# Sharing a router phase's smallest logit among the partitions: through TensorE, or on VectorE alone

## The chip, the cores and the metric

The kernel runs on one core of a Trainium2 chip. The metric is the device time of one execution in microseconds; of three timed runs of the kernel before the median is 709.76 us (707.22 to 710.5). Work is done by TensorE (PE; its weight loads are PEld), VectorE (DVE), ScalarE (ACT), GpSimd (POOL, which issues the gathers and scatters here) and SyncE (SP, which issues the plain loads). Each works through its own instructions in order and waits on semaphores for the others.

## The reference, cut to what matters

Attention with a causal window of 128 and a linear bias feeds a mixture of eight experts. Tokens go to experts greedily by their logits, each expert taking at most `cap` of them.

```python
x = attention(q, k, v)                  # 4608 tokens x 512
logits = x @ w_gate                     # 4608 x 8
cap = N // E                            # 576
for idx in np.argsort(-logits.flatten()):
    tok, e = idx // E, idx % E
    if assigned[tok] >= 0 or counts[e] >= cap: continue
    assigned[tok] = e; counts[e] += 1
for e in range(E):
    h = np.maximum(x[assigned == e] @ w1[e], 0.0)
    out[assigned == e] = h @ w2[e]
```

## The kernel before, in words

The first part (to about 230 us) is the attention, head pair by head pair. It is the same before and after. From then on the experts run one after another on TensorE: `layer1` (L895) multiplies the gathered tokens, split into a high and a low part (`xh`, `xl`), by the first weights; `layer2` (L924, L925, L927) multiplies the result (`hh`, `hlo`) by the second weights into `po`. Beside the matmuls ACT and DVE split each loaded weight piece `raw` into a high and a low part `hl` (L837, L839), DVE makes `hlo` (L906), POOL gathers the next expert's tokens `g` by the indices `idx` (L848) and scatters the output (L936), and TensorE transposes `g` into `pg` (L872), from which ACT and DVE make `xh` and `xl` (L875, L876).

The router does not sort. It runs in phases 0 to 7; each closes one expert. In a phase every token has a best remaining logit `b` (L490 to L497). The phase looks for the threshold above which an expert is full: between the smallest `b` (`lo`) and the last threshold (`hi`) it lays 64 steps of width `w`, marks on DVE for each token which steps it reaches (`ind`, L556, two halves), counts the marks per expert with TensorE (L580), and finds the step at which an expert fills up (L588 to L594, then L597). That is done three times, ever finer. Then come the selection, the places of the chosen tokens (L695, L715, L716) and their list `idx` (L743 to L751). All of it stands between the expert matmuls: `phase` is a generator that yields the number of slots to wait (`WAITS`), and `slot` is called between groups of expert matmuls and takes the route one yield further when the wait is over. So a phase is spread over some twenty slots, and phases run ahead of the experts by about two. The framework's scheduler then sets the final order of each engine's instructions.

The smallest `b` is known only per partition after a reduction along the free axis (L504). `ends` brings it to all partitions: TensorE transposes the column into a row in PSUM (L509), DVE reduces the row to one number (L511), multiplies it into an identity (L513), TensorE multiplies that by ones (L516, two instructions for fp32), and DVE copies the result out and negates it (L518, L520). Two yields lie in it: `WAITS[0]` = 2 slots before L509, `WAITS[1]` = 1 slot before L516. Phases 1 to 6 call it with `top` false; phase 0 calls it once with `top` true, inside the attention, and phase 7 not at all. `EARLY` says how many yields of the route are taken before the first expert's loop starts.

Of the kernel before, what the change touches and what calls it, by code (L numbers as in the profile page):

```python
# [5 lines left out]
F32 = mybir.dt.float32  # L6
# [4 lines left out]
ALU = mybir.AluOpType  # L11
AX = mybir.AxisListType
# [398 lines left out]

CONST_AT = 4
WARM, WARM0, WARM1 = 11, 16, 4
EARLY = 4
AHEAD = (18, 0, 0)
EARLY0 = 1
SOON, HI0 = 2, 1
# [4 lines left out]
WAITS = (2, 1, 3, 1, 1, 2, 3)  # L422
# [13 lines left out]
def bc(ap, shape):  # L436
    return ap.to_broadcast(shape)
# [17 lines left out]
class Router:  # L455
# [43 lines left out]
    def ends(self, b, top):  # L499

        nc, C = self.nc, self.C
        n = 2 if top else 1
        e = self.small("ext", 2)
        nc.vector.tensor_reduce(e[:, 0:1], b, AX.X, ALU.min, negate=True)  # L504
        if top:
            nc.vector.tensor_reduce(e[:, 1:2], b, AX.X, ALU.max)
        yield WAITS[0]
        ep = self.bank()
        nc.tensor.transpose(ep[0:n, 0:128], e[:, 0:n], C["ident"])  # L509
        em = self.p["rt"].tile([2, 1], F32, name="em")  # L510
        nc.vector.tensor_reduce(em[0:n], ep[0:n, 0:128], AX.X, ALU.max)  # L511
        ed = self.p["rt"].tile([2, 2], F32, name="ed")
        nc.vector.tensor_scalar(ed[0:n, 0:n], C["ident"][0:n, 0:n], em[0:n, 0:1], None, ALU.mult)  # L513
        yield WAITS[1]
        ea = self.bank()
        nc.tensor.matmul(ea[:, 0:n], C["onef"][0:n, :], ed[0:n, 0:n], start=True, stop=True)  # L516
        ev = self.small("ev", 2)
        nc.vector.tensor_copy(ev[:, 0:n], ea[:, 0:n])  # L518
        lo = self.small("lo")
        nc.vector.tensor_scalar(lo, ev[:, 0:1], -1.0, None, ALU.mult)  # L520
        if top:

            sp, ab = self.small("sp"), self.small("ab")
            nc.vector.tensor_tensor(sp, ev[:, 0:1], ev[:, 1:2], ALU.add)
            nc.vector.tensor_scalar(sp, sp, 2.0 ** -10, 1e-20, ALU.mult, ALU.add)
            nc.vector.tensor_scalar(ab, ev[:, 1:2], -1.0, ev[:, 1:2], ALU.mult, ALU.max)
            nc.vector.scalar_tensor_tensor(sp, ab, 2.0 ** -20, sp, ALU.mult, ALU.add)
            nc.vector.tensor_tensor(self.hi, ev[:, 1:2], sp, ALU.add)
            yield 0
        w = self.small("w")  # L530
        nc.vector.tensor_scalar(w, self.hi, lo[:, 0:1], 1.0 / J, ALU.subtract, ALU.mult)
        rw = self.small("rw")
        nc.vector.tensor_scalar(w, w, 1e-30, None, ALU.max)
        nc.vector.reciprocal(rw, w)
        return lo, w, rw

    def clamp(self, out, b, lo, w, c0=0, c1=NT):

        low = self.small("low")
        self.nc.vector.tensor_tensor(low, lo, w, ALU.subtract)  # L540
        self.nc.vector.tensor_scalar(out[:, c0:c1], b[:, c0:c1], self.hi[:, 0:1], low[:, 0:1], ALU.min, ALU.max)
# [445 lines left out]
def layer_moe(tc, P, C, r, x, w1, w2, out, exact):  # L987
# [23 lines left out]
    with tc.issue_after(last.ins):  # L1011
        for _ in range(EARLY - EARLY0):
            next(route)
# [130 lines left out]
```

## Time and profile before

| | |
|---|---|
| median of three runs | 709.76 us (707.22 to 710.5) |
| the profiled execution | 710.48 us, of which the span from first to last instruction is 708.7 us |
| PE busy | 677.7 us (96%) |
| DVE busy | 467.5 us (66%) |
| ACT / POOL busy | 330.7 us / 154.1 us |
| mean granted TensorE clock | 0.985 of full speed |
| chain that ended last | PE 88%, DVE 5%, DMA 3% |

The span has three parts: the attention to about 230 us with PE nearly full, a short stretch about 230 to 243 us in which router phase 0 ends and PE has little to do, and the experts from 243 us to the end, in which PE is again nearly full. A busy PE is one whose instructions follow without a gap; a router instruction between two expert matmuls is busy time too.

### The profile page before, as it was taken

What the parts mean: (1) busy time and instruction counts of PE and PEld (TensorE: products, weight loads), DVE (VectorE), ACT (ScalarE), POOL (GpSimd) and SP (SyncE); (2) the same over time, 40 slices, a digit from 0 to 9 for tenths busy, and PEclk for the clock granted to TensorE, in tenths of its full rate; (3) what the DMA queues carried; (4) which work ended last, traced back from release to release, by engine and by line L of the source; (5) the groups of instructions that cost most, each with busy time, mean ns of one, the idle gap of its engine ahead of it and who ended that gap; (6) DMA issues with size and microseconds to landing.
All of it is one profiled execution on the core that took longest, in us unless ns stands there. A gap on an engine that the chain in (4) does not pass through costs nothing.

```text
span 708.7 us, 19210 instructions
## 1 busy us (share of the span) xinstructions
PE 677.7 (96%) x7446; PEld 598.3 (84%) x7447; DVE 467.5 (66%) x1855; ACT 330.7 (47%) x991; POOL 154.1 (22%) x337
## 2 busy tenths in 40 slices
PE   7999999999993799999999999999999999999996
PEld 4998998998892598789788889988988988988986
DVE  6887887888887889689577828846764724523210
ACT  6988888898862343334233224314324324322211
POOL 4121221222130304323140131132034023011011
PEclk9999999999996899999999999999999999999999
DMA  8466565664521634527054235135134334401001
GB/s 304 136 215 188 167 205 170 193 217 151 171 85 38 203 104 163 187 90 239 31 175 151 77 105 179 54 114 175 61 119 132 122 97 139 138 20 40 8 24 49
DMA packets 35140, 92.74 MB, mean 131 GB/s; under 512 B 3808, under 2 KB 13152, under 8 KB 35040
## 3 DMA queue, kind: packets, MB, share of 16 engines
q1 hardware_dynamic: 29152, 72.55, 31.3%
q0 software_dynamic: 5888, 18.88, 8.2%
q8 instruction: 61, 1.00, 0.6%
q14 instruction: 39, 0.32, 0.1%
HBM read 72.54 MB, written 18.87 MB: 129 GB/s over the span
## 4 chain that ended last, share of the span: by engine, by line
PE 88%; DVE 5%; DMA 3%; issue 2%; POOL 1%; ACT 0%; SPq 0%; POOLq 0%; DVEq 0%
PE ph L895 28%; PE po L924 10%; PE po L925 10%; PE s L53 8%; PE po L927 8%; PE pt L53 7%; PE pt L157 6%; PE x L53 5%; PE pg L872 2%; DMA g<-x,idx 2%; PE m L580 1%; DVE u L133 1%; DMA raw<-in_w_dram 1%; DMA out_dram<-o,idx 1%; DMA rel_sb<-in_rel_dram 1%
## 5 line engine op out<-in xcount | busy, mean ns | idle before, releaser
L895 PE MATMUL ph<-xh,hl 128*128 128x288 f32 (+2 forms) x1024 | 193.1, 301 | 0.0
L895 PEld LDWEIGHTS ph<-xh,hl 128*128 128x128 f32 x1024 | 155.5, 190 | 1.0
L144 ACT ACTIVATE u<-u,mn 128x192 f32<-128x192 f32 (+2 forms) x288 | 123.9, 434 | 22.7 <-DVE mn L133 22.7
L924 PE MATMUL po<-hl,hh 128*128 128x512 f32 (+1 forms) x328 | 130.7, 399 | 0.0
L925 PE MATMUL po<-hl,hh 128*128 128x512 f32 (+1 forms) x328 | 126.4, 385 | 0.0
L901 ACT ACTIVATE hh<-ph 128x288 fp32r<-128x288 f32 (+2 forms) x128 | 46.7, 409 | 150.3 <-PE ph L895 141.3
L895 PE MATMUL ph<-xl,hl 128*128 128x288 f32 (+2 forms) x512 | 116.3, 298 | 0.0
L133 DVE CUSTOM_DVE_ANT_0 u<-s,bm 128x192 f32<-128x192 f32 x308 | 86.4, 333 | 30.2 <-PE s L53 29.8
L927 PE MATMUL po<-hl,hlo 128*128 128x512 f32 (+1 forms) x264 | 101.7, 385 | 0.0
L839 DVE TENSOR_TENSOR hl<-raw,hl 128x512 fp32r<-128x512 f32 x128 | 85.1, 684 | 15.2 <-ACT hl L837 14.4
L936 POOL DMA_INDIRECT out_dram<-o,idx x40 | 44.1, 1103 | 205.6 <-ACT o L931 120.8
L895 PEld LDWEIGHTS ph<-xl,hl 128*128 128x128 f32 x512 | 84.8, 190 | 0.1
L876 DVE TENSOR_TENSOR xl<-pg,xh 128x512 fp32r<-128x512 f32 (+1 forms) x37 | 23.7, 640 | 85.7 <-ACT xh L875 78.1
L906 DVE SCALAR_TENSOR_TENSOR hlo<-ph,hh 128x288 fp32r<-128x288 f32 (+2 forms) x128 | 49.6, 417 | 41.3 <-ACT hh L901 40.3
L837 ACT CAST hl<-raw 128x1024 fp32r<-128x1024 f32 x64 | 65.5, 1049 | 16.5 <-DMA raw<-in_w_dram 11.9
L53 PE MATMUL s<-qk 64*64 64x192 f32 (+1 forms) x1112 | 69.5, 319 | 2.8 <-DVE mn L133 2.6
L924 PEld LDWEIGHTS po<-hl,hh 128*128 128x128 f32 x328 | 61.7, 188 | 11.1
L925 PEld LDWEIGHTS po<-hl,hh 128*128 128x128 f32 x328 | 61.8, 188 | 10.7
L931 ACT COPY o<-po 128x512 f32<-128x512 f32 (+1 forms) x33 | 19.0, 574 | 96.5 <-PE po L927 62.5
L848 POOL DMA_INDIRECT g<-x,idx x40 | 44.7, 1119 | 82.5 <-PE pg L872 34.2
L927 PEld LDWEIGHTS po<-hl,hlo 128*128 128x128 f32 x264 | 49.6, 188 | 10.2
L53 PEld LDWEIGHTS s<-qk 64*64 64x64 f32 x1112 | 48.2, 132 | 8.4 <-issue 3.7
(217 smaller groups left out, 936.4 us busy)
## 6 DMA issues: line engine op xcount, KB each, us to landing
raw<-in_w_dram SPq DMA_DIRECT2D x64, 512.0 KB, 4.3
qk<-in_qk_dram SPq DMA_DIRECT2D x32, 576.0 KB, 5.0
v<-in_v_dram SPq DMA_DIRECT2D x32, 288.0 KB, 4.1
x<-xb SPq DMA_DIRECT2D x14, 512.0 KB, 3.4
x<-xb SPq DMA_DIRECT2D x8, 128.0 KB, 2.7
x<-xb SPq DMA_DIRECT2D x4, 256.0 KB, 2.1
g<-x,idx POOLq DMA_INDIRECT x40
out_dram<-o,idx POOLq DMA_INDIRECT x40
```

Of the source, the lines that this page charges most:

```text
L53: put(nc.tensor.matmul(out, w, a, start=start, stop=stop, skip_group_check=True))
L133: put(nc.vector.tensor_tensor_reduce(out=u[rows], in0=x[rows, c:c + 64 * m].rearrange("q (j k) -> q j k", k=64), in1=bm[n % NP][rows, y:y ...
L144: put(nc.scalar.activation(u, u, AF.Exp, bias=st["mn"][:, i:i + 1], scale=-1.0, accum_out=st["sm"][:, i:i + 1]))
L837: self.last = nc.scalar.copy(hl[:, 0, :], raw)
L839: nc.vector.tensor_tensor(hl[:, 1, c:c + 512], raw[:, c:c + 512], hl[:, 0, c:c + 512].bitcast(F32), ALU.subtract)
L848: nc.gpsimd.indirect_dma_start(out=g[:r, :], out_offset=None, in_=self.x, in_offset=bass.IndirectOffsetOnAxis(ap=idx[:r, h:h + 1], axis=0))
L895: nc.tensor.matmul(pp[t], w[:, a, j, fo:fo + 128], x[:, j, cut[t]:cut[t + 1]], start=(j == 0 and a == 0 and x is xh), stop=(j == 3 and a = ...
L901: nc.scalar.activation(o, pp[t], AF.Relu)
L906: nc.vector.scalar_tensor_tensor(d, pp[t][:, c0:c1], 0.0, o[:, c0:c1].bitcast(F32), ALU.max, ALU.subtract)
L924: nc.tensor.matmul(out, a, wh, start=(f == 0), stop=False)
L925: nc.tensor.matmul(out, a, wl, start=False, stop=(f == 7 and t == 4))
L927: nc.tensor.matmul(out, hl[:, f, 128 * t:128 * t + 128], wh, start=False, stop=(f == 7))
```

## The change: what it does

For `top` false, `ends` no longer goes through TensorE. The new `least` reduces `b` to one number per partition, copies it over 32 columns, lets DVE transpose the four 32x32 squares of each 32-partition group in place (so every partition holds the 32 values of its group), reduces again, and then twice takes the minimum with a copy shifted by partitions: first halves of 64 are exchanged (two copies), then quarters of 32 (four copies). The yield `WAITS[1]` is gone with the second TensorE instruction, so that each of the phases 1 to 6 is one yield and one slot shorter; `EARLY` goes from 4 to 3, since the third yield is now where the fourth was. `both_ends` is the old way, for `top` true.

```diff
-EARLY = 4
+EARLY = 3
...
-        n = 2 if top else 1
-        e = self.small("ext", 2)
-        nc.vector.tensor_reduce(e[:, 0:1], b, AX.X, ALU.min, negate=True)
...
-        yield WAITS[0]
-        ep = self.bank()
-        nc.tensor.transpose(ep[0:n, 0:128], e[:, 0:n], C["ident"])
-        em = self.p["rt"].tile([2, 1], F32, name="em")
-        nc.vector.tensor_reduce(em[0:n], ep[0:n, 0:128], AX.X, ALU.max)
-        ed = self.p["rt"].tile([2, 2], F32, name="ed")
-        nc.vector.tensor_scalar(ed[0:n, 0:n], C["ident"][0:n, 0:n], em[0:n, 0:1], None, ALU.mult)
-        yield WAITS[1]
-        ea = self.bank()
-        nc.tensor.matmul(ea[:, 0:n], C["onef"][0:n, :], ed[0:n, 0:n], start=True, stop=True)
-        ev = self.small("ev", 2)
-        nc.vector.tensor_copy(ev[:, 0:n], ea[:, 0:n])
-        lo = self.small("lo")
-        nc.vector.tensor_scalar(lo, ev[:, 0:1], -1.0, None, ALU.mult)
...
+        if not top:
+            lo = self.least(b)
+            yield WAITS[0]
+        else:
+            lo = yield from self.both_ends(b)
...
+    def least(self, b):
+
+        nc, rt = self.nc, self.p["rt"]
+        e, t = self.small("ext"), self.small("ext2", 64)
+        nc.vector.tensor_reduce(e, b, AX.X, ALU.min)
+        nc.vector.tensor_copy(t[:, 0:32], bc(e, [128, 32]))
+        nc.vector.transpose(t[:, 32:64], t[:, 0:32])
+        nc.vector.tensor_reduce(e, t[:, 32:64], AX.X, ALU.min)
+        for w in (64, 32):
+            o, lo = self.small("other"), self.small("lo")
+            for a in range(0, 128, w):
+                nc.vector.tensor_copy(o[a:a + w], e[a ^ w:(a ^ w) + w])
+            nc.vector.tensor_tensor(lo, e, o, ALU.min)
+            e = lo
+        return lo
```

The order of the instructions moves with it from the first expert on. Two places are shown. In the kernel after, line numbers below the new code are higher by 22.

DVE at the start of phase 4, before: `em`, `ed` and `ev` are L511, L513 and L518 of `ends`, `o` is expert 1's last output block, `hl` a split weight, `hlo` and `hh` the first layer of expert 2.

```order
L935 TENSOR_TENSOR o<-po,o_6675 64x512
L511 TENSOR_REDUCE em<-m 1x1
L839 TENSOR_TENSOR hl<-raw,hl 128x512
L513 TENSOR_SCALAR ed<-ident_sb,em 1x1
L839 TENSOR_TENSOR hl<-raw,hl 128x512
L906 SCALAR_TENSOR_TENSOR hlo<-ph,hh 128x288
L906 SCALAR_TENSOR_TENSOR hlo<-ph,hh 128x224
L906 SCALAR_TENSOR_TENSOR hh<-ph,hh 128x64
L518 COPY ev<-m 128x1
L839 TENSOR_TENSOR hl<-raw,hl 128x512
L520 TENSOR_SCALAR lo<-ev 128x1
```

DVE at the start of phase 4, after: `other` and `lo` are L525 and L526 of `least`, `ind` (L578) is what was L556, and `io` (L768) opens the last step of phase 3.

```order
L526 TENSOR_TENSOR lo<-lo,other 128x1
L508 TENSOR_SCALAR w<-hi,lo 128x1
L510 TENSOR_SCALAR w<-w 128x1
L511 RECIPROCAL rw<-w 128x1
L562 TENSOR_TENSOR low<-lo,w 128x1
L665 TENSOR_TENSOR low<-lo,w 128x1
L666 TENSOR_SCALAR w<-w 128x1
L563 TENSOR_SCALAR cl<-b,hi,low 128x36
L667 TENSOR_SCALAR rw<-rw 128x1
L568 TENSOR_SCALAR kq<-cl,lo,rw 128x72
L578 TENSOR_TENSOR ind<-kq,c_i_425 128x1152 x2
L768 COPY io<-m 64x20
```

The marks of phase 4 have moved from behind expert 2's first `hlo` to ahead of the last step of phase 3, two experts' stretches of work earlier than their count.

PE at the start of the same phase, before: the first layer of expert 2 (`ph`) with the transpose L509 and the multiplication L516 in it.

```order
L895 MATMUL ph<-xh,hl 128x288 x2
L509 MATMUL m<-ident_sb,ext 1x128
L895 MATMUL ph<-xh,hl 128x288 x2
L895 MATMUL ph<-xl,hl 128x288 x2
L895 MATMUL ph<-xh,hl 128x288 x4
L895 MATMUL ph<-xl,hl 128x288 x2
L895 MATMUL ph<-xh,hl 128x288 x2
L516 MATMUL m<-ed,craw 128x1
```

PE there after: the same layer is L917, and the first count is L602 (it was L580).

```order
L917 MATMUL ph<-xh,hl 128x288 x4
L917 MATMUL ph<-xl,hl 128x288 x2
L917 MATMUL ph<-xh,hl 128x288 x4
L917 MATMUL ph<-xl,hl 128x288 x2
L917 MATMUL ph<-xh,hl 128x288 x2
L602 LDWEIGHTS ind
```

The two router instructions are gone from the row, and 48 matmuls of the layer stand ahead of the first count, where it was 12, 12 and 41 before.

## Rows read from the trace of the kernel before

**Rows 1.** The page, busy time, and granted clock in 40 slices.

```profile
PE 677.7 (96%) x7446; PEld 598.3 (84%) x7447; DVE 467.5 (66%) x1855; ACT 330.7 (47%) x991; POOL 154.1 (22%) x337
PEclk9999999999996899999999999999999999999999
```

**Rows 2.** Busy time by stretches: PE, PEld, DVE, ACT, POOL, clock, DMA, GB/s.

```profile
300.00:340.00 40.00, 39.21 (x333) 35.70 (x332) 34.88 (x118) 14.32 (x26) 10.76 (x10) 1.00 0.44 146
```

**Rows 3.** Line L509: count, duration (min/median/max), first and last start.

```profile
L509 PE MATMUL m<-ident_sb,ext x6: 271/271/272, 242.9 to 487.4; 128*1 128x128 f32 x6
```

**Rows 4.** Timeline of PEld at L509 (phase 3) and L516 (phases 1, 5).

```profile
323.54 0.08 PEld L509 LDWEIGHTS m<-ident_sb,ext 128*1 128x1 f32 x1
323.67 0.30 PEld L895 LDWEIGHTS ph<-xh,hl 128*128 128x128 f32 x2
...
244.44 0.19 PEld L895 LDWEIGHTS ph<-xh,hl 128*128 128x128 f32 x1
...
245.07 0.19 PEld L895 LDWEIGHTS ph<-xl,hl 128*128 128x128 f32 x1
...
430.87 0.19 PEld L895 LDWEIGHTS ph<-xh,hl 128*128 128x128 f32 x1
431.30 0.29 PEld L516 LDWEIGHTS m<-ed,craw 1*128 1x128 f32 x2 [0.24 <-DVE ed L513]
431.61 0.19 PEld L895 LDWEIGHTS ph<-xh,hl 128*128 128x128 f32 x1
```

**Rows 5.** Timeline of PEld at phase 2, up to the transposes of expert 1's tokens.

```profile
279.69 0.19 PEld L927 LDWEIGHTS po<-hl,hlo 128*128 128x128 f32 x1
279.92 0.08 PEld L509 LDWEIGHTS m<-ident_sb,ext 128*1 128x1 f32 x1
...
284.56 0.42 PEld L872 LDWEIGHTS pg<-ident_sb,g 128*128 128x128 f32 x4 [1.83 <-DMA g<-x,idx]
```

**Rows 6.** Timeline of POOL at the gather for expert 1.

```profile
277.25 1.44 POOL L848 DMA_INDIRECT g<-x,idx  x1 [5.87 <-issue]
278.99 3.27 POOL L848 DMA_INDIRECT g<-x,idx  x1 [0.30 <-issue]
```

**Rows 7.** Timeline of DVE at the start of phase 4.

```profile
370.34 0.20 DVE L513 TENSOR_SCALAR ed<-ident_sb,em 1x1 f32<-1x1 f32 x1
...
372.72 0.46 DVE L906 SCALAR_TENSOR_TENSOR hlo<-ph,hh 128x288 fp32r<-128x288 f32 x1 [1.58 <-ACT hh L901]
...
373.87 0.15 DVE L518 COPY ev<-m 128x1 f32<-128x1 f32 x1
...
375.76 0.15 DVE L643 TENSOR_TENSOR low<-lo,w 128x1 f32<-128x1 f32 x1
375.83 0.15 DVE L644 TENSOR_SCALAR w<-w 128x1 f32<-128x1 f32 x1
...
377.06 1.42 DVE L556 TENSOR_TENSOR ind<-kq,c_i 128x1152 bf16<-128x1152 bf16 x2
```

**Rows 8.** Timeline of PEld at phase 4's first count.

```profile
377.86 0.33 PEld L580 LDWEIGHTS <-ind 128*128 128x128 bf16 x9 [1.48 <-DVE ind L556]
```

**Rows 9.** PE after that wait: length, busy time, clock, DMA share, GB/s.

```profile
379.60:383.00 3.40, 3.40 (x16) 0.50 0.47 151
```

**Rows 10.** Timeline of PE in and after that stretch.

```profile
380.40 1.16 PE L895 MATMUL ph<-xh,hl 128*128 128x288 f32 x4
381.36 0.68 PE L895 MATMUL ph<-xl,hl 128*128 128x288 f32 x2
...
384.20 0.69 PE L895 MATMUL ph<-xh,hl 128*128 128x288 f32 x4
384.72 0.42 PE L895 MATMUL ph<-xl,hl 128*128 128x288 f32 x2
```

**Rows 11.** Timeline of PEld at the places of phase 2's tokens.

```profile
315.09 0.10 PEld L715 LDWEIGHTS <-c_ones 128*128 128x128 bf16 x1 [1.03 <-DVE ex L712]
```

**Rows 12.** DVE, 243 to 709 us, by line: busy us, mean ns, idle before.

```profile
L496 DVE TENSOR_REDUCE am<-cand 128x36 bf16<-128x288 bf16 x6 | 4.0, 668 | 0.0
```

More of the change, by code (lines that the diff above doesn't have):

```diff
@@ L501, in ends @@
         nc, C = self.nc, self.C
-        n = 2 if top else 1
-        e = self.small("ext", 2)
-        nc.vector.tensor_reduce(e[:, 0:1], b, AX.X, ALU.min, negate=True)
-        if top:
-            nc.vector.tensor_reduce(e[:, 1:2], b, AX.X, ALU.max)
-        yield WAITS[0]
-        ep = self.bank()
-        nc.tensor.transpose(ep[0:n, 0:128], e[:, 0:n], C["ident"])
-        em = self.p["rt"].tile([2, 1], F32, name="em")
-        nc.vector.tensor_reduce(em[0:n], ep[0:n, 0:128], AX.X, ALU.max)
-        ed = self.p["rt"].tile([2, 2], F32, name="ed")
-        nc.vector.tensor_scalar(ed[0:n, 0:n], C["ident"][0:n, 0:n], em[0:n, 0:1], None, ALU.mult)
-        yield WAITS[1]
-        ea = self.bank()
-        nc.tensor.matmul(ea[:, 0:n], C["onef"][0:n, :], ed[0:n, 0:n], start=True, stop=True)
-        ev = self.small("ev", 2)
-        nc.vector.tensor_copy(ev[:, 0:n], ea[:, 0:n])
-        lo = self.small("lo")
-        nc.vector.tensor_scalar(lo, ev[:, 0:1], -1.0, None, ALU.mult)
[L521 to L529, printed above, removed]
+        if not top:
[3 more added lines that the diff above has]
+            lo = yield from self.both_ends(b)
         w = self.small("w")
@@ L535, in ends, with both_ends @@
         return lo, w, rw
+    def least(self, b):
[12 more added lines that the diff above has]
+        return lo
+    def both_ends(self, b):
+        nc, C = self.nc, self.C
+        e = self.small("ext", 2)
+        nc.vector.tensor_reduce(e[:, 0:1], b, AX.X, ALU.min, negate=True)
+        nc.vector.tensor_reduce(e[:, 1:2], b, AX.X, ALU.max)
+        yield WAITS[0]
+        ep = self.bank()
+        nc.tensor.transpose(ep[0:2, 0:128], e, C["ident"])
+        em = self.p["rt"].tile([2, 1], F32, name="em")
+        nc.vector.tensor_reduce(em, ep[0:2, 0:128], AX.X, ALU.max)
+        ed = self.p["rt"].tile([2, 2], F32, name="ed")
+        nc.vector.tensor_scalar(ed, C["ident"][0:2, 0:2], em[:, 0:1], None, ALU.mult)
+        yield WAITS[1]
+        ea = self.bank()
+        nc.tensor.matmul(ea[:, 0:2], C["onef"][0:2, :], ed, start=True, stop=True)
+        ev = self.small("ev", 2)
+        nc.vector.tensor_copy(ev, ea[:, 0:2])
+        lo = self.small("lo")
+        nc.vector.tensor_scalar(lo, ev[:, 0:1], -1.0, None, ALU.mult)
+        sp, ab = self.small("sp"), self.small("ab")
+        nc.vector.tensor_tensor(sp, ev[:, 0:1], ev[:, 1:2], ALU.add)
+        nc.vector.tensor_scalar(sp, sp, 2.0 ** -10, 1e-20, ALU.mult, ALU.add)
+        nc.vector.tensor_scalar(ab, ev[:, 1:2], -1.0, ev[:, 1:2], ALU.mult, ALU.max)
+        nc.vector.scalar_tensor_tensor(sp, ab, 2.0 ** -20, sp, ALU.mult, ALU.add)
+        nc.vector.tensor_tensor(self.hi, ev[:, 1:2], sp, ALU.add)
+        yield 0
+        return lo
     def clamp(self, out, b, lo, w, c0=0, c1=NT):
```

## The prediction

> **What bounds the kernel now.** I read the page's busy times first: PE is busy 96% of the span, DVE 66% [rows 1]. So the question is what the change gives or costs TensorE, and each idle stretch of PE counts. The clock row of the page comes next: its 6 and its 8 are the stretch ahead of the experts, where PE has little to do; a second fall from 2.4 GHz is too short to show in that row and appears in the table by stretches [rows 9]. Then I went through the waits of PE and of its weight loads from 243 us on, and found four that are long: at phase 2's gather [rows 5], at phase 2's places [rows 11], at phase 4's first count [rows 8], and the router's own small instructions [rows 4]. Everywhere else the expert matmuls follow each other at their own pace. DVE is busiest in the stretch 300 to 340 us, 34.9 of 40 us [rows 2], which holds most of phases 2 and 3.
>
> **What goes from TensorE.** `ends` with `top` false runs in phases 1 to 6, so L509 runs six times [rows 3] and L516 twelve times. The durations of these instructions (271 ns) are no price, since matmuls overlap; the price is what they add between the weight loads of two expert matmuls.
> - L509 takes one place in the row: its load starts at 323.54, the next expert load at 323.67, so 0.13 us [rows 4].
> - L516 stands between loads at 430.87 and 431.61, 0.74 us apart, where an undisturbed first-layer step is 0.13 (four of them from 384.20 to 384.72, [rows 10]). It costs 0.61, of which 0.24 is a wait for DVE's `ed` [rows 4]. Phases 4, 5 and 6 have the same picture. In phase 1 it is 245.07 less 244.44, less a step of 0.13: 0.50 [rows 4]; I take that for phase 3 as well.
> - Phase 2 is left out here: what follows its L516 waits for a gather (below).
>
> Sum of this term: 5 x 0.13 + 3 x 0.61 + 2 x 0.50 = 3.5 us. Its bounds are 0, if PE runs into the same DVE or DMA earlier and waits there, and 3.5.
>
> **Phase 2's gather.** TensorE waits 1.83 us for expert 1's tokens, to 284.56 [rows 5]. What it saves ahead of that point in phases 1 and 2 beyond what the indices come earlier is lost in this wait. In phase 1 I found DVE's chain, not PE's, to lead towards the end: the new order puts `b` of the next phase ahead of `hif`, but takes two waiting `hlo` from ahead of it, so I let it end unchanged or up to 0.3 us earlier. The new order has 29 instead of 27 second-layer matmuls of a row between the indices' last matmul and the transposes; at 0.23 each (279.69 to 279.92, [rows 5]) 0.46 us of work has moved into the wait. Against that, `idx` has a reduction of the next phase ahead of it where it had a shorter comparison, which I put at 0.25 us. I take a gain of 0.2 us, bounds -1 and +0.7.
>
> **Phase 4's first count.** This is the part that the diff does not tell. Before, `ed` is done at 370.5, but `ev` runs only at 373.87, since DVE takes its instructions in order and two halves of `hlo` stand between them, waiting for expert 2's first layer on ACT [rows 7]. So `ind` starts at 377.06, and PE, which wants it for the count, waits 1.48 us [rows 8]. From 379.6 to 383.0 PE then runs with a granted clock of 0.5, that is at 1.2 GHz [rows 9]: four matmuls take 0.96 us (380.40 to 381.36) instead of 0.52 [rows 10]. Some 14 matmuls lie in that stretch; at 0.24 instead of 0.13 they cost 1.5 us. In the new order `least` needs nothing of PE, and all of it down to both halves of `ind` stands ahead of the last step of phase 3. The count has moved forward by 17 matmuls (48 instead of 65 ahead of it in the layer), 2.2 us (17 x 0.13), but its marks by a whole stretch of expert 1's second layer. So the wait goes. That the low clock goes with it I infer from its place, right behind the only long PE wait of the neighbourhood. Gain: 1.5 + 1.5 = 3.0 us; bounds 0 (another late mark or another cause of the clock) and 3.0.
>
> **Phase 2's places.** PE waits 1.03 us for `ex` (L712) [rows 11], behind a DVE row of `hlo` and of the next phase's `b`. In the new order `ex` comes ahead of `b` (a reduction like that of [rows 12], 0.67 us), but PE has 19 instead of 24 matmuls to cover it, 0.65 us less, and one first-layer `hlo` pair moved to behind the sum. I take half of the wait, 0.5 us, as gained; bounds -0.6 and 1.0.
>
> **What DVE gets.** Twelve instructions of a phase (two reductions, a broadcast copy, a transpose, two and four copies, two minima) for five before: seven more. The trace has no DVE transpose and no copy across partitions. From below: independent one-column instructions start 0.07 us apart (375.76 and 375.83, [rows 7]). From above: the slowest router reduction, 0.67 us, of 128x288 [rows 12]. I take 0.15, the duration of the one-column instructions [rows 7], which are nearest in size, so about 1 us more a phase (0.5 to 6, with five old ones gone). In 300 to 340 us DVE has 5.1 us idle for parts of two phases [rows 2], so 2 us are hidden there, and in the other stretches more. What is queued behind them on DVE is `hlo`, which `layer2` needs a layer later, and the first `xl` of expert 0 at 242 us, which I expect one or two of the small instructions later, 0.15 to 0.3 us.
>
> **New waits.** Some counts and sums stand closer: in phases 4 to 6 the sum L695 follows L597 by 7 matmuls (0.9 us) instead of 13, and phase 1's first count has 36 matmuls ahead instead of 40. I set aside 0.8 us; bounds 0 and 3.0, the price of one more case like phase 4's.
>
> **Sum.** 3.5 + 0.2 + 3.0 + 0.5 - 0.8 = 6.4 us. Against the profiled execution's own 710.48 us (span 708.7 and 1.8 around it) that is 704.1 us. The median of the runs shown, 709.76, is 0.7 lower than the profiled one, so I round to 704.0, 5.8 us or 0.8% below that median.
>
> **A rule on the gather.** POOL's second index list for expert 1 took 3.27 us to issue, the first 1.44 [rows 6], while DVE ran `hl` after `hl`. The Trainium skill, "SBUF — State Buffer", section "Who interferes with whom", says that a DVE copy in a two-port mode and a GpSimd instruction exclude each other for a whole instruction, and that descriptors of a GpSimd DMA are held up by that. The change puts seven copies beside this gather, so by that rule expert 1's tokens could land up to 7 x 0.15 = 1 us later, and the sum would be 705.1 instead of 704.1. The slow issue agrees with a lock, though the same section infers that a two-input DVE operation, which `hl` is, does not hold descriptors up; I give the copies' lock a chance of its own.
>
> **The rivals.**
> 1. One wait goes, another comes. With the order reshuffled, PE meets some other late DVE result for about 1.5 us and again runs some microseconds at 1.2 GHz, so the 3.0 us come back elsewhere. For it: DVE runs in order, and any `hlo` that waits for ACT blocks the router behind it, as in phase 4. Against it: in the new order the marks stand ahead of the layers they were stuck behind. Time: 710.5 - 3.5 - 0.2 + 0.3 = 707.1.
> 2. PE's time is hidden anyway. Each phase ends at the pace of DVE and the gathers, and what PE saves becomes waits at L597, L695 or L715, with the phase 4 wait replaced as in rival 1. For it: PE does wait for DVE in every phase, by tenths. Against it: the expert matmuls, not the router, fill the row, and phases run two experts ahead. Time: 709.5.
> 3. The copies' lock on the gather: 705.1.
> 4. Slower: DVE becomes the bound in 300 to 340 us. If the twelve instructions cost more than some 0.4 us each (a transpose or a copy across partitions that drains the engine), the seven more and the five dearer ones together pass the 5.1 us that DVE has left there [rows 2]. At the upper bound of 0.67 each a phase gets about 7 us more, 14 in two phases, of which 9 would appear on PE through late `hlo` and marks, less 3.5 for PE: 716. Decides from about 0.4 us an instruction. Against it: the rows of one-column instructions are all near 0.15.
>
> That the change would not do what it says I exclude by the order: L509 and L516 are absent from PE's row in phases 1 to 6.
>
> **How the numbers follow.** Forecast 0.62, with its own range of 701.5 to 706.2; rival 1 0.18; rival 2 0.07; rival 3 0.05; rival 4 0.08. A difference of 0.5% (about what a measurement of this kernel can tell from no change) is 3.5 us, so faster means below 706.2. Faster: 0.95 of the forecast, all of rival 3, a third of rival 1: 0.70. Slower: rival 4 and a small rest, 0.09. Same: 0.21. The low end adds the upper bounds of the gather and of the places to the sum and drops the new waits, 710.5 - 3.5 - 0.7 - 3.0 - 1.0 = 702.3, and another 1.5 for a run that is fast by itself, as one of the three shown was: 700.8. The high end takes rival 1 and most of rival 2: 709.0. Left out: rival 4 and parts of the two.
>
> **What would show it.** In the profile after: no L509 or L516 on PE after 243 us; the weight loads of first-layer steps 0.13 apart where they stood; no wait at phase 4's first count and no stretch at 0.5 between 360 and 400 us; the wait at expert 1's transposes still there and within 1 us of 1.83; DVE's new instructions near 0.15 us and DVE's busy time up by some 6 us. The forecast is wrong if the half clock shows up behind a new PE wait (rival 1), if PE's waits for DVE in 243 to 560 us grow by more than 2 us (rival 2), or if the transpose or the copies take more than 0.4 us (rival 4).

## The result and the profile after

The changed kernel takes 711.01 us (median of 18 runs, 709.09 to 716.53), the kernel before on the same chip 708.04 us (18 runs, 706.19 to 711.32). The ratio is 1.0035, with an interval of [1.002, 1.0049]: 3.0 us slower, where 704.0 us, some 6 faster, were forecast. The profiled execution took 710.70 us (span 708.9).

TensorE's work did shrink, DVE's grew by forty-two instructions, and PE's share of the span fell. First the page after (busy time, and granted clock in 40 slices), beside [rows 1]:

```profile
PE 674.6 (95%) x7429; PEld 595.1 (84%) x7429; DVE 469.8 (66%) x1897; ACT 330.5 (47%) x991; POOL 147.1 (21%) x337
PEclk9999999999996899999999999999999999999998
```

Then the new instructions, by line, with count, busy time, mean ns and idle time before them, from 240 to 600 us of the trace after (one record of some lines is missing):

```profile
L525 DVE COPY other<-lo 32x1 f32<-32x1 f32 x24 | 3.5, 145 | 0.4
...
L525 DVE COPY other<-ext 64x1 f32<-64x1 f32 x12 | 1.8, 149 | 0.3
...
L520 DVE STREAM_TRANSPOSE ext<-ext 128x32 f32<-128x32 f32 x6 | 1.2, 201 | 0.0
...
L526 DVE TENSOR_TENSOR lo<-lo,other 128x1 f32<-128x1 f32 x6 | 0.9, 157 | 0.1
...
L518 DVE TENSOR_REDUCE ext<-b 128x1 f32<-128x36 f32 x5 | 0.9, 182 | 0.0
...
L519 DVE COPY ext<-ext 128x32 f32<-128x32 f32 x5 | 0.9, 171 | 0.0
```

All are between 145 and 201 ns: the price of 0.15 us was about right, so rival 4 (0.4 us each and more) is out. Where does PE lose time, then? In its waits. The waits of the weight loads from 242 to 545 us (total, times, longest), first after, then in a second profile of the kernel before, whose L580, L597 and L715 are L602, L619 and L737 now:

```profile
PEld L737 <- DVE ex L734: 4.3, 5, 1.0
PEld L602 <- DVE ind L578: 2.7, 4, 1.1
PEld L619 <- DVE sat L616: 2.4, 3, 1.9
```
```profile
PEld L715 <- DVE ex L712: 1.8, 4, 1.0
PEld m L516 <- DVE ed L513: 1.1, 4, 0.4
...
PEld L597 <- DVE sat L594: 1.0, 6, 0.2
PEld L580 <- DVE ind L556: 1.0, 3, 0.3
```

In the rows shown 9.4 us of waits on DVE stand against 4.9; with the smaller rows left out here it is 11.9 against 7.1 (7.5 in the first profile of the kernel before). Three of the new ones are alike, at the places of phases 4, 5 and 6 (timeline of PEld, start, duration; what it waited for in brackets):

```profile
397.49 0.10 PEld L737 LDWEIGHTS <-c_ones 128*128 128x128 bf16 x1 [1.02 <-DVE ex L734]
...
455.57 0.10 PEld L737 LDWEIGHTS <-c_ones 128*128 128x128 bf16 x1 [1.01 <-DVE ex L734]
...
513.69 0.10 PEld L737 LDWEIGHTS <-c_ones 128*128 128x128 bf16 x1 [1.02 <-DVE ex L734]
```

Most of what I had looked at ahead is as foretold or better: phase 4's first count has no wait [rows 8] (its marks now start 13.1 us ahead of it, at 361.38 us), no stretch near it is at half clock [rows 9], the places of phase 2 wait 0.63 instead of 1.03 us [rows 11], and the tokens of expert 1 are waited for 0.73 instead of 1.83 us [rows 5]:

```profile
282.77 0.31 PEld L894 LDWEIGHTS pg<-ident_sb,g 128*128 128x128 f32 x3 [0.73 <-DMA g<-x,idx]
...
314.36 0.10 PEld L737 LDWEIGHTS <-c_ones 128*128 128x128 bf16 x1 [0.63 <-DVE ex L734]
```

Two of the checks that I had named failed: the wait at expert 1's transposes is 1.10 us from 1.83 where I had allowed 1, though on the good side, and DVE's busy time rose by 2.3 us, not by some 6. (The durations alone are as foretold: from 238 us on the twelve new instructions take 11.5 us in all six phases, the five old ones 5.6; busy time counts overlapping instructions once.) And one named sign of being wrong came, waits for DVE up by more than 2 us. Three things explain the time: some of what went had not been there to take, new waits came behind the step that I had looked at, and the spread on DVE is not free.

**A quieter measure than the whole time.** The 18 runs of one kernel spread over 5 to 7 us, and much of that is spent outside the change (last section). For the profiles I therefore also use the time from the first weight load of one expert's first layer to that of the next. Five such stretches, e0 to e4, hold phases 2 to 6 and most of phase 1. Each row is one execution, and e0 differs by up to 0.9 us between executions of one kernel, e2 to e4 by less than 0.05 but for the 60.71. In us, from the traces ("second slot" and the rest are the experiments below):

```
kernel               e0     e1     e2     e3     e4     sum
before, 1st profile  64.37  59.66  60.71  57.95  57.86  300.55
before, 2nd          63.48  59.78  57.84  57.94  57.84  296.88
before, 3rd          63.59  59.77  57.84  57.94  57.84  296.98
after, 1st           65.00  60.04  58.09  58.11  58.14  299.38
after, 2nd           65.26  59.94  58.06  58.09  58.11  299.46
second slot          63.77  59.92  57.59  57.35  57.08  295.71
 + TensorE's two     64.25  60.00  57.93  57.92  57.68  297.78
 no least            63.20  59.71  57.07  57.19  57.08  294.25
 least twice         67.28  60.70  58.82  57.37  57.08  301.25
 WAITS[5] = 3        64.10  59.49  57.91  57.16  57.17  295.83
before, slot off     64.72  59.87  58.98  58.99  58.97  301.53
after, WAITS[5] = 3  64.79  59.88  57.06  57.04  57.06  295.83
 WAITS[0] = 3 too    65.91  61.29  57.07  57.04  57.06  298.37
 WAITS[3] = 2 too    68.84  58.79  60.41  59.11  57.36  304.51
```

### The profile page after: what moved, and what is told of

Same layout as the page of the kernel before. It is cut to its first block, busy times and chain, and to the rows that moved or that the text cites. A ratio compares the mean times of both kernels' runs of the same rounds, so it can differ in the third digit from the quotient of the medians.

```text
span 708.9 us, 19219 instructions
## 1 busy us (share of the span) xinstructions
PE 674.6 (95%) x7429; PEld 595.1 (84%) x7429; DVE 469.8 (66%) x1897; ACT 330.5 (47%) x991; POOL 147.1 (21%) x337
## 4 chain that ended last, share of the span: by engine, by line
PE 84%; DVE 8%; DMA 4%; issue 1%; ACT 1%; SPq 0%; POOL 0%; POOLq 0%; DVEq 0%
PE ph L917 25%; PE po L946 10%; PE po L947 9%; PE s L53 8%; PE po L949 7%; PE pt L53 7%; PE pt L157 6%; PE x L53 6%; PE pg L894 2%; DMA raw<-in_w_dram 1%; PE m L602 1%; DMA craw<-in_cst_dram 1%; DVE hl L861 1%; DVE hlo L928 1%; DMA qk<-in_qk_dram 1%
## 5 line engine op out<-in xcount | busy, mean ns | idle before, releaser
L917 PE MATMUL ph<-xh,hl 128*128 128x288 f32 (+2 forms) x1024 | 189.9, 299 | 0.0
L917 PEld LDWEIGHTS ph<-xh,hl 128*128 128x128 f32 x1024 | 154.0, 189 | 1.2 <-DVE hlo L928 0.4
L917 PE MATMUL ph<-xl,hl 128*128 128x288 f32 (+2 forms) x512 | 115.6, 297 | 0.0
L958 POOL DMA_INDIRECT out_dram<-o,idx x40 | 41.4, 1036 | 217.3 <-ACT o L953 123.8
L917 PEld LDWEIGHTS ph<-xl,hl 128*128 128x128 f32 x512 | 84.3, 189 | 0.2
L870 POOL DMA_INDIRECT g<-x,idx x40 | 40.8, 1020 | 88.7 <-PE pg L894 43.2
```

The source lines that it names most:

```text
L917: nc.tensor.matmul(pp[t], w[:, a, j, fo:fo + 128], x[:, j, cut[t]:cut[t + 1]], start=(j == 0 and a == 0 and x is xh), stop=(j == 3 and a = ...
```

## The experiments

Theory 1: the spread on DVE pays as forecast, and the loss comes from the slot that went with the yield. Theory 2: the seven more DVE instructions of a phase cost what TensorE gained. Theory 3: TensorE's instructions were hidden anyway. The kernel before ran on the same chip beside each of the three groups of kernels, with medians of 708.73, 708.99 and 708.81 us; each ratio is to its own group's. Beside the result it was 708.04, so a difference between medians of different groups is good to about 1 us only.

**Two more profiles of the kernel before.** The prediction booked 3.0 us for a wait and a half clock at phase 4. No edit here.

> The kernel before once more, for a second profile. Theory 1 and 2 alike: if the wait of 1.5 us at the first count of phase 4 and the half clock behind it belong to this kernel, they are there again (377.86 in the first profile); if they belonged to that one execution, phases 4 to 6 read alike, about 57.9 us each or less, and the 3.0 us that the prediction booked for them was not there to be taken.

> The kernel before, third profile. If the wait of 1.5 us at the first count of phase 4 and the half clock behind it are this kernel's, they are there in most of its executions; if they came by that one execution, phase 4 takes about 57.9 us again, as in the second.

They took 707.42 and 709.54 us (one run each, on two chips). In both, phase 4's stretch e2 is 57.84 us, like e3 and e4. The first count starts without a wait (second profile, PEld) where [rows 8] has 1.48 us, and PE runs at 2.4 GHz behind it (length, PE, PEld, DVE, ACT, POOL, clock, DMA, GB/s) where [rows 9] has 0.50:

```profile
375.39 0.10 PEld L580 LDWEIGHTS <-ind 128*128 128x128 bf16 x1
```
```profile
375.40:380.00 4.60, 4.60 (x49) 4.34 (x47) 4.23 (x17) 0.71 (x2) 0.00 (x0) 1.00 0.47 159
380.00:384.00 4.00, 4.00 (x46) 3.92 (x45) 3.52 (x9) 1.65 (x3) 0.00 (x0) 1.00 0.12 49
```

So that wait belonged to one execution. Why `hh` came 1.8 us late on ACT in it, with DMA's share at 1.03 to 1.08 in the same stretch, the traces don't show. The same holds for phase 2's gather: the two profiles wait 0.61 and 0.78 us there, not 1.83.

**After, second profile.**

> The kernel after, second profile. Theory 1 (lost slot): the waits of 1.2 us at L737 in phases 4 to 6 are there again, 58.1 us each phase. Theory 2 says nothing else here.

709.02 us, one run. The three waits are there again (weight loads 1.2 us apart at 397.26, 455.31, 513.40), and the five stretches differ from the first profile by 0.08 us in sum. The waits belong to the kernel. By the stretches the change costs 299.4 - 296.9 = 2.5 us, by the medians 3.0.

**The second slot kept**, with `least` on DVE:

```diff
-EARLY = 3
+EARLY = 4
             yield WAITS[0]
+            yield WAITS[1]
```

> VectorE spreads the smallest logit as in the kernel after, but the yield WAITS[1] stands where it stood and EARLY is 4, so the phases take the slots they took before; in PE's row only L509 and L516 are missing against the kernel before. Theory 1 (the lost slot costs, the spread itself pays): 3 to 4 us faster than before, ratio 0.994 to 0.997, no wait of 1 us at the places' sums of phases 4 to 6. Theory 2 (the seven more VectorE instructions cost): as slow as the kernel after, ratio 1.002 to 1.005. Theory 3 (TensorE's instructions were hidden anyway): like before, 0.999 to 1.001.

708.22 us (12 runs), ratio 1.001 [0.999, 1.003]: 2.8 us below the changed kernel, 3.7 by the stretches. By the ratios, each to its own group, the difference is 1.8 us. The slot's loss is most of the result, but Theory 1's figure was missed: with the slot restored nothing that can be told is gained on before. The figure is Theory 3's (0.999 to 1.001); its reason, that TensorE's instructions were hidden, is tested below. Phase 4's places, PEld of this kernel and DVE of the kernel after:

```profile
395.08 0.19 PEld L947 LDWEIGHTS po<-hl,hh 128*128 128x128 f32 x1
...
396.83 0.19 PEld L950 LDWEIGHTS po<-hl,hlo 128*128 128x128 f32 x1
397.28 0.10 PEld L738 LDWEIGHTS <-c_ones 128*128 128x128 bf16 x1 [0.26 <-DVE ex L735]
```
```profile
393.57 0.46 DVE L719 TENSOR_REDUCE Dc<-m 128x8 f32<-128x288 f32 x1 [0.66 <-PE m L717]
393.95 0.74 DVE L928 SCALAR_TENSOR_TENSOR hlo<-ph,hh 128x288 fp32r<-128x288 f32 x2
394.61 0.21 DVE L928 SCALAR_TENSOR_TENSOR hh<-ph,hh 128x64 fp32r<-128x64 f32 x1
394.74 0.16 DVE L722 SCALAR_TENSOR_TENSOR keyv<-Dc,left 128x8 f32<-128x8 f32 x1
...
397.28 0.16 DVE L734 TENSOR_TENSOR ex<-run,m 128x36 bf16<-128x36 bf16 x1
```

These rows show two halves of one mechanism. In the kernel after, the sum (L717) has moved one slot earlier, and DVE's group `hlo`, `hlo`, `hh`, which used to run ahead of the sum, falls between `Dc` and `keyv`: `ex` starts 3.71 us behind `Dc`, against 3.07 with the second slot (393.95 to 397.02). And PE has 24 first-layer matmuls of 0.13 us between the sum and the places (3.1 us), where it had 11 of these and 9 second-layer ones of 0.23 (3.5 us; the nine from 395.08 to 396.83 above).

**The slot taken away alone**, with TensorE's old way (lines one lower than after):

```diff
-EARLY = 4
+EARLY = 3
-        yield WAITS[1]
+        if top:
+            yield WAITS[1]
```

> The smallest logit goes through TensorE as before, but the yield WAITS[1] is gone and EARLY is 3, so the phases are one slot shorter as in the kernel after. Theory 1: slower than before by what the slot costs in the kernel after plus the TensorE instructions, 4 to 7 us, ratio 1.006 to 1.010, with waits of about 1 us at the places' sums (L715) of phases 4 to 6. Theory 2: like before or faster, ratio 0.997 to 1.001, since no VectorE work is added. Theory 3: ratio 1.002 to 1.005, the whole loss of the kernel after.

713.16 us (8 runs), ratio 1.006 [1.0033, 1.0087], 4.4 us over before: as Theory 1 said, against Theories 2 and 3. The same wait stands at the same place:

```profile
398.39 0.10 PEld L716 LDWEIGHTS <-c_ones 128*128 128x128 bf16 x1 [1.02 <-DVE ex L713]
...
457.40 0.10 PEld L716 LDWEIGHTS <-c_ones 128*128 128x128 bf16 x1 [1.01 <-DVE ex L713]
```

**The changed kernel with a longer stretch ahead of the places.**

```diff
-WAITS = (2, 1, 3, 1, 1, 2, 3)
+WAITS = (2, 1, 3, 1, 1, 3, 3)
```

> The kernel after with one slot more between ex and the sums of the places (WAITS[5] 3 instead of 2). Theory 1: the waits of 1 us at L715's place in phases 4 to 6 go, about 0.75 each, so 2 to 2.5 us faster than the kernel after, ratio to before 0.999 to 1.002; waits of the first phases stay. Theory 2: as slow as the kernel after, 1.002 to 1.005. Theory 3: as after, or slower.

708.37 us (12 runs), ratio 0.9997 [0.9981, 1.0014]: 2.6 us below the changed kernel, as Theory 1 said. PE now has the 24 and 9 second-layer matmuls in between, and the waits at L737 are down to 0.26; e2 to e4 take 57.05 us each, 1.05 less than after. So the three stretches give back 3.1 us together, of which 0.76 each, 2.3 us, is the wait at the places itself. The loss there is one of cover, not of DVE's load, since DVE's instructions are the same.

**TensorE's two instructions put back, unused**, into the version with the second slot:

```diff
             yield WAITS[0]
+            ep = self.bank()
+            self.nc.tensor.transpose(ep[0:1, 0:128], C["ident"][:, 0:1], C["ident"])
             yield WAITS[1]
+            ea = self.bank()
+            self.nc.tensor.matmul(ea[:, 0:1], C["onef"][0:1, :], C["ident"][0:1, 0:1], start=True, stop=True)
```

> The first of these kernels with one transpose and one multiplication of the old shapes put back on TensorE at the old slots, on constants, and their results used by nobody: the price of these instructions alone. Theory 1: 2 to 3.5 us slower than the first kernel (six times 0.13 and six times 0.4, the old 0.6 without its wait for ed), so near the kernel before, ratio 0.998 to 1.001. Theory 2: like the kernel after or slower, 1.003 to 1.008. Theory 3: the same time as the first kernel within 0.5 us.

710.95 us (12 runs), ratio 1.0026 [1.0007, 1.0046]. That is 2.7 us over the version without them by the medians and 2.1 by the stretches. By the ratios it is 1.1 us. The two intervals overlap, so the size is known only to about 2 us, but Theory 3 is out: the stretches show 0.3 to 0.6 us in four of the five. Theory 1's difference (2 to 3.5 us) came, its ratio (0.998 to 1.001) did not. The forecast's first term was 3.5, with DVE's `ed` waited for; these instructions run on constants and wait for nothing.

**The smallest logit left out**: a constant below all logits stands for it, in the version with the second slot.

```diff
-            lo = self.least(b)
+            lo = self.small("lo")
+            self.nc.vector.memset(lo, -0.5)
```

> The version with the second slot kept, with the smallest logit left out (a constant below all logits stands for it). Theory 1 (what VectorE's spread costs is small, the loss lies in slots): as the version with the second slot, 0.998 to 1.001 of before. Theory 2 (the eleven VectorE instructions in each phase cost 2 to 3 us, which eats what TensorE's two gave): 0.995 to 0.997.

705.35 us (12 runs), ratio 0.9952 [0.9934, 0.997], as Theory 2 said: 2.9 us below the version with the spread by the medians, 4.1 by the ratios, 1.5 by the stretches. So the spread on DVE is not free, and it eats about what TensorE's two instructions gave. By the two profiles the loss lies in e0 to e2 (0.57, 0.21, 0.52), little of it in e3 (0.16) and none in e4; the 0.57 is no more than e0 differs between executions of one kernel. The trace after shows how the spread is drawn out in a first phase. DVE in phase 2:

```profile
276.56 0.18 DVE L518 TENSOR_REDUCE ext<-b 128x1 f32<-128x36 f32 x1
276.66 0.68 DVE L861 TENSOR_TENSOR hl<-raw,hl 128x512 fp32r<-128x512 f32 x1
277.26 0.18 DVE L519 COPY ext<-ext 128x32 f32<-128x32 f32 x1
277.34 0.69 DVE L861 TENSOR_TENSOR hl<-raw,hl 128x512 fp32r<-128x512 f32 x1
277.95 0.21 DVE L520 STREAM_TRANSPOSE ext<-ext 128x32 f32<-128x32 f32 x1
...
278.71 0.31 DVE L525 COPY other<-ext 64x1 f32<-64x1 f32 x2
279.06 0.69 DVE L861 TENSOR_TENSOR hl<-raw,hl 128x512 fp32r<-128x512 f32 x1
...
280.45 0.62 DVE L525 COPY other<-lo 32x1 f32<-32x1 f32 x4
281.10 0.69 DVE L861 TENSOR_TENSOR hl<-raw,hl 128x512 fp32r<-128x512 f32 x1
281.71 0.15 DVE L526 TENSOR_TENSOR lo<-lo,other 128x1 f32<-128x1 f32 x1
```

Twelve instructions with 1.9 us of work take 5.3 us, because after each dependent step the order puts an `hl` or `hlo` of 0.4 to 0.7 us. DVE is never idle meanwhile, yet what follows in the route waits all the same.

**The spread done twice**, a second pass over the first one's result, in the version with the second slot:

```diff
             lo = self.least(b)
+            lo = self.least(lo)
```

> The version with the second slot, with VectorE's eleven instructions of the spread done twice in each phase (the second copy's result unused by nothing else than the first's place). Theory 2 (the spread's instructions cost 2 to 3 us by their number): 2 to 3 us over the version with it once, 1.004 to 1.006 of before. Theory 1 (they lie in cover; what is lost is by the order that results in the first three phases): phases 5 and 6 as with one, 57.1 to 57.4 us each, and the time within 1.5 us of the version with one, 0.999 to 1.003.

710.77 us (12 runs), ratio 1.0039 [1.0018, 1.006]: 2.6 us over the version with one. Each theory is half right. e3 and e4 stay as they were (57.37, 57.08), so there the instructions lie in cover; e0 to e2 grow by 3.5, 0.8 and 1.2 us. The order of these three phases changes too, and in this execution TensorE's granted clock is 0.50 (1.2 GHz) from 285.1 to 288.4 us, at the end of a long wait for a gather. At half clock 3.3 us do the work of 1.65, so by this estimate about half of the 3.5 us is the clock's, and none of it is the price of an instruction. The largest waits of this kernel, at a gather and at a count of phase 3:

```profile
285.22 0.18 PEld L896 LDWEIGHTS pg<-ident_sb,g 128*128 128x128 f32 x1 [3.11 <-DMA g<-x,idx]
...
337.18 0.10 PEld L604 LDWEIGHTS <-ind 128*128 128x128 bf16 x1 [1.37 <-DVE ind L580]
```

**Three tries for a faster version.** First the second slot with the longer stretch ahead of the places:

```diff
-EARLY = 3
+EARLY = 4
-WAITS = (2, 1, 3, 1, 1, 2, 3)
+WAITS = (2, 1, 3, 1, 1, 3, 3)
             yield WAITS[0]
+            yield WAITS[1]
```

> The version with the second slot kept and WAITS[5] at 3. Theory 1: no wait at L737 was lost in it, so nothing is won in phases 4 to 6: 0.998 to 1.002. Theory 2: as the version with the second slot, 1.001.

706.68 us (12 runs), ratio 0.9964 [0.9948, 0.998]: below both kernels, by the medians 2.3 us under before and 4.3 under after, and the best of the kernels that compute everything. Both theories had it at 0.998 or above. Its stretches sum to 295.83, no better than with the second slot alone (295.71), so the 1.5 us between these two medians, which come from different groups, are not explained by the routes and not shown to be the edit's.

Then the changed kernel with `WAITS` at (3, 1, 3, 1, 1, 3, 3):

> After, with WAITS[0] and WAITS[5] both 3. Theory 1: the waits of 1.2 us at L737 in phases 4 to 6 go as with WAITS[5] alone, and a longer first stretch in phases 1 to 3 takes the waits of some 0.8 to 2 us at the counts and at L619 there: 0.995 to 0.999. Theory 2: 0.999 to 1.002, as with WAITS[5] alone, since the same VectorE instructions stand there.

710.16 us (12 runs), ratio 1.0018 [1.0001, 1.0034]: a miss for Theory 1, and within Theory 2's figure though not for its reason. Phases 4 to 6 keep their 57.05 us, while e0 and e1 take 65.91 and 61.29. In e0 TensorE waits 2.75 us for expert 1's gather, and its granted clock is 0.50 from 286.7 to 290.0 us, which by the same estimate costs some 1.65 us by itself; in e1 it waits 2.13 us for `xl` ahead of transposes. So the longer early stretch did not take the early waits away; how much of e0 is the edit's and how much this execution's is not shown, since the profiled run (712.84 us) is the slowest of the twelve. At last (2, 1, 3, 2, 1, 3, 3):

> After, with WAITS[3] at 2 and WAITS[5] at 3, so that 24 matmuls stand where 12 to 17 did around the counts of phases 4 to 6. Theory 1: no waits at L737 and as few as in the version with WAITS[5] alone: 0.996 to 1.000. Theory 2: 0.999 to 1.002.

712.08 us (11 runs), ratio 1.0053 [1.0034, 1.0073], a miss for both. In the profiled execution, at 716.13 us the slowest of the eleven, the gather for expert 1 is late, and the granted clock is 0.50 from 289.7 to 296.4 us:

```profile
290.52 0.18 PEld L894 LDWEIGHTS pg<-ident_sb,g 128*128 128x128 f32 x1 [5.07 <-DMA g<-x,idx]
```

Phase 1's route is longer here, which may be why; but the stretches of this profile are 8.7 us over those of the kernel with `WAITS[5]` alone and the medians only 3.7, so not all of it is in every execution.

## Why the prediction was wrong

The steps of the sum, in us (gains positive):

```
step of the prediction      forecast   by stretches   by medians
TensorE's L509, L516          +3.5        +2.1           +2.7
phase 2's gather              +0.2         0              0
phase 4's first count         +3.0         0              0
phase 2's places              +0.5      (+0.4, in new waits)
DVE's instructions             0          -1.5           -2.9
new waits (the lost slot)     -0.8        -3.7           -2.8
sum                           +6.4        -3.1           -3.0
the change itself                         -2.5           -3.0
```

The first, fifth and sixth rows come from the version with the second slot against the same with TensorE's two, without `least`, and after. The gather and the places are read from their waits (0.73 us after, 0.61 and 0.78 before; 0.63 after, 1.03 before). The 0.4 us at phase 2's places came with the shorter route and not with the spread: the wait is 1.02 with the second slot, and 0.62 with TensorE's way and the slot off. So it lies in the last difference already. The steps are not wholly independent, so the table is a balance, not a proof of each line to a tenth; by the ratios the three measured rows are 1.1, -4.1 and -1.8. The 0.6 us between sum and change by the stretches may be the waits for `ed` (1.1 us in the rows above), which the unused instructions don't have; no run shows that.

**The step that failed first is phase 4's first count.** The wait was read rightly from [rows 7, 8] and the half clock from [rows 9, 10], and the new order removes the order of DVE that I blamed. But e3 and e4 ran through the same order of instructions in the same trace and had no such wait: 57.95 and 57.86 us against 60.71 for e2. A wait that one of three like phases has may be a mark of that execution alone, and two further profiles show that this one was. The profiled execution stood 2.4 us above the median of the 18 runs beside the result, about as much as the excess of e2, 2.9 us. Without this step the sum was 3.4 us instead of 6.4. That the low clock belonged to the wait I had inferred from its place. Elsewhere the length of a wait alone doesn't tell: behind this one of 1.48 us the clock fell, while the granted clock stays 1.00 from 243 to 560 us with waits of 1.88 (after), 2.07 (after with `WAITS[5]` at 3) and 2.26 us (with the second slot too), and it falls to 0.50 beside gather waits of 2.75, 3.11 and 5.07 us (the variants with `WAITS[0]` at 3, `least` twice and `WAITS[3]` at 2).

**New waits were sized wrong, with the place next to the right one in sight.** I saw that in phases 4 to 6 the sum now follows the count by 7 matmuls instead of 13, asked whether the sum would wait, and set aside 0.8 us with a bound of 3.0. The sum doesn't wait. The next step does, since what left the stretch ahead of the sum entered the one behind it on DVE (0.8 us of `hlo` and `hh`), and its own cover fell from 3.5 to 3.1 us. It does so in all three phases: 0.76 us more each, 2.3 us in all, and a longer stretch there gave 3.1 us back. e0 lost another 1.2 to 1.5 us with the slot. The term measured 3.7 us by the stretches, above its bound of 3.0, and 2.8 by the medians. With 3.7 in place of 0.8 the sum is down to 0.5 us, no change that can be told.

**DVE was costed at nothing because its idle time was larger than the new work.** The duration was right and the cover was not the question: in 300 to 340 us DVE is busy 35.0 us, hardly more than in [rows 2], and yet TensorE is busy 38.7 us instead of 39.2. The term measured 1.5 us by the stretches and 2.9 by the medians. What counts is when the last of a dependent row of instructions is done, with unrelated ones in between. With this term too, the sum is below zero.

**TensorE's term was right in kind and perhaps a little large**, 2.1 to 2.7 of 3.5. Part of its gaps was cover for DVE, as the bound of 0 allowed: phase 3's first count waits 0.79 us in the version with the second slot and 0.37 with TensorE's two put back. Another part was the wait for `ed`, which the unused instructions leave out.

**The rivals.** Rival 2 (PE's saving becomes waits for DVE) named the mark that came true, waits on DVE up by more than 2 us: by 4.5 in the rows shown. It named L597, L695 and L715 as the places; two of the three are right. Its 709.5 missed the median by 1.5, since it let the waits eat the gain and no more. Rival 1's new half clock did not come in the kernel after; three of the variants' profiles have one. Rival 3 is out: POOL's second issue for expert 1 takes 0.95 us now, with the new copies on DVE beside it, against 3.27 in [rows 6]:

```profile
277.05 1.22 POOL L870 DMA_INDIRECT g<-x,idx  x1 [7.98 <-issue]
278.56 0.95 POOL L870 DMA_INDIRECT g<-x,idx  x1 [0.30 <-issue]
```

The rule of the Trainium skill, "SBUF — State Buffer", section "Who interferes with whom", that a copy in a two-port mode holds descriptors up, thus has no price here; these copies are of one column, and whether they run in such a mode no run here shows. The issue of 3.26 to 3.27 us stands in all three profiles of the kernel before and in the one with the slot off, and in none with `least` or with the constant (0.95 to 1.31 us); why it is slow in the old order stays open.

**What stays open.** The waits of phases 1 to 3 move from place to place with each edit: e0 has 1.88 us at L619 after, 2.21 at a transpose with `least` left out, 2.26 at a gather with the second slot and `WAITS[5]` at 3. The wait at L619 is not the slot's: it is 2.03 us with the second slot, 2.08 with TensorE's two beside it, and none of the profiles of the kernel before has one over 0.36 there. That `least` costs some 1.5 to 4 us is measured; how it is shared among the phases and which of its instructions decides is not.

## What to carry to other kernels

Removing a yield together with its instruction is two changes: it also takes cover from every later step of the route, and the cover was worth about as much here as the instructions or more (3.7 us against 2.1 by the stretches, 2.8 against 2.7 by the medians). Before a gain is booked on a wait, look for the same wait in the sister phases of the same trace; where it stands in one of them alone, take a second profile. Here phase 4's wait was gone in it, while the 1.03 us at phase 2's places, in one phase alone too, stood in all three. And when work moves to an engine with idle time, follow the dependent row through that engine's order, with what stands between, not the sum of its durations.

## What the runs showed of the hardware

- A spread over 128 partitions on DVE by a 32x32 transpose (201 ns) and one-column copies shifted by 32 or 64 partitions (145 to 149 ns) takes twelve instructions and 1.9 us of busy time. The shifted copies don't overlap: in the rows of phase 2 above two take 0.31 and four 0.62 us, 0.16 each, where independent one-column instructions start 0.07 apart in [rows 7]. The Trainium skill, "VectorE: DVE Perf Modes", section "Two Vector instructions with no wait between them", says that an instruction whose operand starts in another group of 32 partitions than its predecessor's begins only when all earlier ones are done; these rows agree with it.
- Executions of one kernel differ ahead of the experts: the first load of expert 0's first layer stands at 242.88 and 242.59 us in two profiles of the kernel before and at 245.63 in the third, which alone of the three has a low granted clock at 12 to 24 us (first profile, then third):

```profile
12.00:18.00 6.00, 4.45 (x64) 3.48 (x64) 4.05 (x24) 6.00 (x27) 2.17 (x11) 1.00 0.84 295
18.00:24.00 6.00, 5.86 (x134) 5.19 (x133) 5.37 (x33) 5.87 (x26) 0.23 (x1) 1.00 0.59 167
```
```profile
12.00:18.00 6.00, 4.01 (x48) 3.11 (x51) 3.22 (x18) 6.00 (x27) 1.94 (x11) 0.63 0.90 313
18.00:24.00 6.00, 6.00 (x127) 5.11 (x123) 4.84 (x28) 4.05 (x19) 0.00 (x0) 0.80 0.38 121
```

  Ahead of that, from 6 to 12 us, TensorE is busy 3.77 us in the first and 5.18 in the third. The third's first load is 2.8 us later without any change of the kernel. Three profiles of the variants have the same low clock (0.60 to 0.63 at 12 to 18 us) and first loads at 244.53, 245.30 and 245.43 us.
- From the last expert's first load to the end the profiles of the kernel before take 57.29, 58.55 and 57.17 us, though TensorE's part is the same, 51.7 us each: the last scatter lands at different times.
